# Attention and gated MLP on one core: the first load of q in two halves, the two constants in one, and one store per tile of the last product

## The chip, the core and the metric

The kernel runs on one core of a Trainium2 chip. The metric is the device time of one execution in microseconds (us), as the median of several runs. Three runs of the kernel before gave 281.07, 280.37 and 281.18 us: a median of 281.07.

## What is computed

Eight batches of eight heads, 576 tokens, head width 64. Each head does a linear attention whose features are the positive part of q and k, times a cosine and a sine of the position. The result, 4,608 rows of 512, goes through a two-layer network with the gate h·cos(h).

```python
theta = np.pi / 2.0 * pos / S
phi = concatenate([relu(x) * cos(theta), relu(x) * sin(theta)])    # for q and for k
kv = einsum('bhsf,bhsd->bhfd', k_p, v);  z = sum(k_p, axis=2)
x = (q_p @ kv) / (q_p @ z + 1e-6)       # -> rows of 8 heads x 64
h = x @ w_in                            # 512 -> 2048
out = (h * cos(h)) @ w_out              # 2048 -> 512
```

Inputs and output are float32; the products run on float16 tiles.

## The kernel before

**Tokens.** 576 tokens are four and a half tiles of 128. A batch is therefore read in two pieces (`tokens`, L321): 320 tokens as 64 partitions of five tokens ("five"), and 256 tokens as 64 partitions of four ("four"). The two pieces go to the even and the odd partitions of one tile of 128 partitions (`blocks`, L217). The fifth tokens of all eight batches are collected and form a ninth block of 512 rows. So there are nine blocks, c = 0 to 8; the last is written by `store` and `store_tile` in their branch for c == B.

**The order of the work** is not decided by a scheduler at run time. Each step (a few matmuls, one activation, one DMA) is added to a plan (`Plan.add`). `Plan.run` (L179) sorts the steps by the numbers of a table, `STARTS`, and takes the engine of each from a string, `ENGS`. Each engine then runs its own steps in that order, and waits on semaphores where a tile is written by another engine or by a DMA. The numbers themselves are no times on the chip: only the order that they give counts.

**The start.** `setup` (L1023) issues two small DMAs from ACT: `CS` (L1030), the cosines and sines, 128 partitions of 24 float32, and `IDENT` (L1031), the identity for transposes on TensorE, 128 x 128 float16. SP issues the loads of batch 0 in the order q, k, v (`load`, L330): for q the "four" piece for all eight heads (L340), then the "five" piece (L337), the same for k, and v in two groups of four heads. `prep` (L359) turns a tile of q or k into its features on DVE or ACT, with one column of `CS` as the scale; `q_pe` (L422) transposes on TensorE against `IDENT`. Until there is data TensorE runs warm-up matmuls (`warm`, L1038). A tiny copy on POOL that reads a finished q feature releases the weight loads: first two quarters of w_in (L1071), later the other two, then two quarters of w_out (L1094). The loads of batch 1 wait for the third quarter of w_in through another tiny copy on POOL (`hold_raw`, L1097), and the other two quarters of w_out wait for q of batch 1 (`part_of_w_out`, L1103).

**The middle.** `layer1` does x @ w_in and the gate, `layer2` the product with w_out. For most blocks both are done by a scheme with seven products in place of eight, with sums of the operands made on DVE; L954 is the matmul of `layer2`, L737 that of the fast part of `layer1`.

**The end.** `layer2(8)` (L915) has its last product in two banks of PSUM, one per tile of 128 rows (L1015). Its two results are added to what is there by DVE (L1018, one instruction per tile), the second tile first in the order of the plan, and each is stored by `store_tile` (L859). A tile's 128 partitions hold two batches, 64 partitions each, which lie apart in the output. `store_tile` therefore issues two DMAs for a tile, one from SP and one from ACT, each of 64 partitions x 256 float32 (64 KB). Before them `store` (L824) puts out 512 KB and 256 KB in the same way, half from SP and half from ACT.

Of the kernel before, what the change touches and what calls it, by code (L numbers as in the profile page):

```python
# [17 lines left out]
OPT = dict(F16=0, WS2=[3, 1], HQ=[2, 0, 1], AQ=0, FW=[20, 4, 4, 4, 4], W2F=0, WQ=2, L2F=0, WFI=None, XPE=[0,  # L18
           1, 2, 3, 4], FAST1={3: 2, 4: 2, 5: 2, 6: 4, 7: 4, 8: 4}, MODE={}, HH='', LD=[['k', 0], ['v', 0],
           ['q', 0], ['k', 1], ['v', 1], ['q', 1]], NB=[['A0', 'A1'], ['A0', 'A1', 'M0']], XB=[['B3'], ['B3',  # L20
           'M1']], W0=5, W1=6, WF=[[2, 2, 2, 2], [2, 2, 0, 0]], HOLD=['k', 1], P0=0, RAW1=2, WO2=1, H1=0,
           DA=0, W2=0, SQ=0, NUZ=1)
# [169 lines left out]
def kernel(  # L192
# [9 lines left out]
    nc = tc.nc  # L202
# [32 lines left out]
    def sb(name, shape, dt=F16):  # L235
        return pool.tile(shape, dt, name=name)
# [1231 lines left out]
```

## Time and profile before

| | us |
|---|---|
| median of three runs | 281.07 |
| the profiled execution | 280.38 |
| its span, first to last instruction | 278.5 |
| TensorE busy in it | 271.0 (97%) |
| VectorE (DVE) busy | 236.8 (85%) |
| ScalarE (ACT) busy | 210.2 (75%) |
| GpSimd (POOL) busy | 83.3 (30%) |

The profiled execution is 1.9 us longer than its span, and 0.7 us below the median of the runs. The granted TensorE clock was 0.996. The chain of waits goes back from the last instruction to what released it, step by step, and so lists the pieces that add up to the span. "SPq" and "ACTq" are the issue queues of those engines: a DMA stands there with the time that its issue takes, while its bytes move later. The table of stretches gives, for a stretch of time, the busy time of every engine, the granted clock, the busy share of the 16 DMA engines (a little over 1 where packets overlap) and the bytes moved per second.

### The profile page before, as it was taken

The numbers are of one execution on the slowest core, as the hardware profiler recorded it, in microseconds if no ns is written. First come the engines' busy times: TensorE is split into PE (matmuls) and PEld (weight loads), VectorE is DVE, ScalarE is ACT, GpSimd is POOL, SyncE is SP. The second block draws the span as 40 slices with busy tenths as digits, with TensorE's granted clock in tenths as the row PEclk, the third lists the DMA queues.
The fourth block names the chain that finished last, engine by engine and source line by source line (L and its number), as shares of the span: only waits on it lengthen the run. The fifth ranks groups of instructions, "written<-read, shape, count | busy, mean of one in ns | idle before, by whom it ended". The sixth has DMA issues, their size and how long they took to land.

```text
span 278.5 us, 6813 instructions
## 1 busy us (share of the span) xinstructions
PE 271.0 (97%) x2689; PEld 214.4 (77%) x2689; DVE 236.8 (85%) x442; ACT 210.2 (75%) x363; POOL 83.3 (30%) x104
## 2 busy tenths in 40 slices
PE   8999999999999999999999999999999999999993
PEld 3568766778966677868876878789988888888882
DVE  1886798989999999999999998899989879973952
ACT  2847797979997896888989978995758596777330
POOL 1340020111403001610430045132634372499210
PEclk9999999999999999999999999999999999999998
DMA  6999999999999999969999998939756494698125
GB/s 206 337 206 207 359 230 269 327 311 206 366 253 232 243 259 238 275 209 238 272 269 236 224 259 274 134 88 147 158 75 136 109 166 92 158 141 121 75 78 151
DMA packets 80223, 58.03 MB, mean 208 GB/s; under 512 B 43200, under 2 KB 77248, under 8 KB 80192
## 3 DMA queue, kind: packets, MB, share of 16 engines
q1 hardware_dynamic: 68960, 39.99, 61.1%
q0 software_dynamic: 10496, 17.04, 29.3%
q10 hardware_dynamic: 736, 0.57, 0.7%
q8 instruction: 21, 0.34, 0.5%
q14 instruction: 10, 0.08, 0.1%
HBM read 36.75 MB, written 11.80 MB: 174 GB/s over the span
## 4 chain that ended last, share of the span: by engine, by line
PE 87%; DMA 5%; DVE 3%; ACT 1%; SPq 1%; issue 1%; POOL 0%; DVEq 0%; ACTq 0%
PE M L954 35%; PE M L737 14%; PE M L609 11%; PE TR L737 6%; DMA qm<-in_q_dram 5%; PE M L576 5%; PE M L879 4%; PE ATT L465 3%; PE ATT L398 3%; PE TR L609 2%; PE ATT L1042 1%; DVE KQ L370 1%; PE M L429 1%; ACT ch L548 1%; SPq L340 1%
## 5 line engine op out<-in xcount | busy, mean ns | idle before, releaser
L954 PEld LDWEIGHTS <-gT 128*128 128x128 f16 x560 | 53.9, 98 | 8.3
L954 PE MATMUL M<-w_out_sb,gT 128*128 128x256 f16 x448 | 57.1, 273 | 0.0
L550 DVE TENSOR_TENSOR gT<-M,ch 128x512 f16<-128x512 f32 x73 | 48.5, 685 | 6.6 <-ACT ch L548 6.5
L548 ACT ACTIVATE ch<-M 128x512 f32<-128x512 f32 x75 | 43.4, 596 | 12.1 <-PE M L576 5.0
L369 ACT ACTIVATE KQ<-km,CS 128x512 f16<-128x512 f32 x57 | 38.5, 719 | 0.4 <-DMA km<-in_k_dram 0.4
L965 ACT ACTIVATE ost<-M 128x512 f32<-128x512 f32 x41 | 24.3, 596 | 17.9 <-PE M L954 12.9
L369 ACT ACTIVATE KQ<-qm,CS 128x512 f16<-128x512 f32 x46 | 31.5, 720 | 4.1 <-DMA qm<-in_q_dram 4.1
L609 PE MATMUL M<-xT,w_in_sb 128*128 128x512 f16 x136 | 33.8, 379 | 0.0
L954 PE MATMUL M<-T,S 128*128 128x256 f16 x256 | 32.4, 273 | 0.0
L385 POOL CAST V<-vm 128x1024 f16<-128x1024 f32 (+1 forms) x18 | 15.9, 906 | 50.7 <-DVE den L482 23.8
L737 PEld LDWEIGHTS <-w_in_sb 128*128 128x128 f16 x288 | 27.3, 98 | 4.8 <-issue 0.4
L576 PE MATMUL M<-xT,w_in_sb 128*128 128x256 f16 x256 | 30.4, 273 | 0.2
L954 PEld LDWEIGHTS <-S 128*128 128x128 f16 x256 | 24.8, 98 | 4.1 <-DVE S L930 0.2
L576 PEld LDWEIGHTS <-w_in_sb 128*128 128x128 f16 x256 | 24.4, 98 | 4.1 <-issue 0.5
L749 DVE TENSOR_TENSOR Z<-M,Z 128x512 f32<-128x512 f32 x31 | 21.1, 687 | 4.3 <-PE M L737 3.1
L609 PEld LDWEIGHTS <-w_in_sb 128*128 128x128 f16 x160 | 14.9, 98 | 12.2
L550 POOL TENSOR_TENSOR gT<-Z,ch 128x512 f16<-128x512 f32 x5 | 6.3, 1268 | 56.6 <-ACT ch L548 20.0
L486 DVE TENSOR_TENSOR XN<-ATT,rec 128x512 f16<-128x512 f32 x32 | 22.1, 691 | 1.1
L465 PEld LDWEIGHTS <-qT 128*128 128x128 f16 (+1 forms) x320 | 14.8, 101 | 5.2 <-issue 3.2
L760 ACT ACTIVATE ch<-Z 128x1024 f32<-128x1024 f32 x12 | 12.7, 1057 | 6.9 <-DVE Z L749 4.9
L745 ACT ACTIVATE Z<-M 128x512 f32<-128x512 f32 x26 | 15.1, 596 | 3.4 <-PE M L737 2.4
L370 DVE TENSOR_SCALAR KQ<-qm,CS 128x512 f16<-128x512 f32 x26 | 12.1, 487 | 5.6 <-DMA qm<-in_q_dram 5.6
(152 smaller groups left out, 520.0 us busy)
## 6 DMA issues: line engine op xcount, KB each, us to landing
out_dram<-ost POOLq DMA_DIRECT2D x38, 256.0 KB, 4.3
qm<-in_q_dram SPq DMA_DIRECT2D x8, 640.0 KB, 6.0
km<-in_k_dram SPq DMA_DIRECT2D x8, 640.0 KB, 7.4
qm<-in_q_dram SPq DMA_DIRECT2D x8, 512.0 KB, 6.3
km<-in_k_dram SPq DMA_DIRECT2D x8, 512.0 KB, 6.0
vm<-in_v_dram SPq DMA_DIRECT2D x6, 640.0 KB, 6.1
vm<-in_v_dram SPq DMA_DIRECT2D x6, 512.0 KB, 4.6
w_in_sb<-in_moe_w_in_dram POOLq DMA_DIRECT2D x4, 512.0 KB, 8.1
```

The costliest lines, as they stand in the source:

```text
L369: fn = {"ACT": lambda: nc.scalar.activation(out=out_, in_=in_, func=AF.Relu, scale=sc), "DVE": lambda: nc.vector.tensor_scalar(out=out_, i ...
L385: "POOL": lambda: nc.gpsimd.tensor_copy(out=out_, in_=in_)}
L465: nc.tensor.matmul(bank[hb][ps, hh * D1:(hh + 1) * D1], lhsT=x[:, h, :], rhs=z[:, h, :], start=True, stop=True)
L486: nc.vector.tensor_tensor(out=split(x16[n][:, hs, :], k), in0=A[:, :, :, 0:D], in1=split(rec[n][:, hs], k).unsqueeze(3).broadcast_to((P, k ...
L548: act(0.5, due, lambda: nc.scalar.activation(out=ch[c], in_=bank, func=AF.Sin, bias=math.pi / 2.0, scale=1.0), [key], [("ch", c)])
L550: mul(due, 0.61, lambda q: q.tensor_tensor(out=dst, in0=bank if len(dst.shape) == 2 else bank.rearrange("p (j s) -> p j s", j=dst.shape[1] ...
L576: nc.tensor.matmul(M1[m][:, jj * 2 * P:(jj + 1) * 2 * P], lhsT=w_in_sb[:, cc, j * P:(j + 1) * P], rhs=X[:, cc, ts], start=(cc == 0), stop= ...
L609: nc.tensor.matmul(M, lhsT=w_in_sb[:, cc, j * P:(j + 1) * P], rhs=X[:, cc, :], start=(cc == 0), stop=(cc == NCT - 1))
L737: nc.tensor.matmul(bank[0][:, j * TH:(j + 1) * TH], lhsT=a(cc, j), rhs=b[:, cc, :], start=(first and j == 0 and cc == 0), stop=(last and j ...
L749: dve(0.61, due + 0.3, lambda: nc.vector.tensor_tensor(out=dst, in0=bank[0], in1=dst, op=ALU.add), [bank[1], key], [key])
L954: nc.tensor.matmul(bank[0][:, tt * MH:(tt + 1) * MH], lhsT=a[:, j, tt * P:(tt + 1) * P], rhs=b[:, j, :], start=(first and (apart or tt == ...
L965: act(0.5, due, lambda: nc.scalar.activation(out=dst, in_=view(bank), func=AF.Copy), [bank[1]], dk)
```

## The change

There are three edits, and a table `STARTS` with other numbers for them.

- The cosines, sines and the identity become one tensor, `CONST`, of 128 partitions x 88 float32 (the identity as 64 of them, read as float16), loaded by one DMA. `CS` and `IDENT` are views of it.
- The "four" piece of q of batch 0 is loaded by two DMAs of four heads each (256 KB) in place of one of eight heads (512 KB). The "five" piece follows as before.
- `store_tile` issues one DMA for the 128 partitions of a tile (128 KB), whose destination is two batches x 64 rows x 256. The second tile's goes out from SP, the first tile's from ACT.

The option `L0S` is off, so the new loop over `cuts` in `layer2_plain` has a single cut and does what was there. The new `STARTS` and `ENGS` put the instructions of every engine in the same order as before, but for the DMAs of the three edits: SP issues one more at the start, ACT one fewer at the start, and SP and ACT one fewer each at the end. POOL's queue, with the loads of w_in and w_out in it, has the same entries in the same order.

```diff
-OPT = dict(F16=0, ..., WQ=2, ..., WO2=1, ...)
+OPT = dict(TM=1, CM=0, QS=1, F16=0, ..., L0S=0, ..., WQ=2, ..., WO2=1, ...)
...
-    cs_dr = nc.inline_tensor(cs_np, name="cs_const")
-    ident_dr = nc.inline_tensor(np.eye(P, dtype=np.float16), name="ident_const")
+    CW = cs_np.size // P
+    const_np = np.concatenate([cs_np.reshape(P, -1), np.eye(P, dtype=np.float16).view(np.float32)], axis=1)
+    const_dr = nc.inline_tensor(np.ascontiguousarray(const_np), name="const")
...
-    CS = sb("CS", [P, 2, 2, NT + 2], F32)
-    IDENT = sb("IDENT", [P, P])
+    CONST = sb("CONST", [P, CW + P // 2], F32)
+    CS = CONST[:, 0:CW].rearrange("p (n g t) -> p n g t", n=2, g=2)
+    IDENT = CONST[:, CW:CW + P // 2].bitcast(F16)
...
+            elif b == 0 and nm == "q" and OPT["QS"]:
+                def go4s(h, four):
+                    return lambda: LQ.dma_start(out=blocks(m, 1 - n)[:, h, 0:NT, :], in_=four[:, h])
+                for hs_ in HALVES:
+                    pl.add(LE, LO, 0, due, go4s(hs_, four), (), [(x, 1 - n) for x in part[hs_]],
+                           dma=(nb * NT / 2, 355.0), lane="first", late=LATE_BY[0], lazy=None)
...
     def store_tile(o, i, due):
+        if OPT["TM"]:
+            dst = out.rearrange("(i n s) m -> n i s m", n=2, s=S)[:, 2 + i, 0:S5, 0:MH]
+            put(due, dst.rearrange("n (p t) m -> n p t m", t=NT + 1)[:, :, NT],
+                ost[o][:, i, 0:MH],
+                [("ost", o, 0, i)], *((nc.sync, "SP") if i else (nc.scalar, "ACT")), nb=131.0)
+            return
         for n in range(2):
             dst = out.rearrange("(i n s) m -> n i s m", n=2, s=S)[n][2 + i, 0:S5, 0:MH]
...
-        nc.scalar.dma_start(out=CS, in_=cs_dr.ap())
-        nc.scalar.dma_start(out=IDENT, in_=ident_dr.ap())
+        nc.scalar.dma_start(out=CONST, in_=const_dr.ap())
```

More of the change, by code (lines that the diff above doesn't have):

```diff
@@ L15 @@
 SYNC = mybir.DependencyInfo(mybir.DependencyClass.Sync, mybir.DependencyReason.DATA)
[L18 to L22, printed above, removed]
@@ L25 @@
-STARTS = (
[98 rows of a table removed]
+OPT = dict(TM=1, CM=0, QS=1, F16=0, WS2=[3, 1], HQ=[2, 0, 1], AQ=0, L0S=0, FW=[20, 4, 4, 4, 4], W2F=0, WQ=2,
+           L2F=0, WFI=None, XPE=[0, 1, 2, 3, 4], FAST1={3: 2, 4: 2, 5: 2, 6: 4, 7: 4, 8: 4}, MODE={}, HH='',
+           LD=[['k', 0], ['v', 0], ['q', 0], ['k', 1], ['v', 1], ['q', 1]], NB=[['A0', 'A1'], ['A0', 'A1',
+           'M0']], XB=[['B3'], ['B3', 'M1']], W0=5, W1=6, WF=[[2, 2, 2, 2], [2, 2, 0, 0]], HOLD=['k', 1],
+           P0=0, RAW1=2, WO2=1, H1=0, DA=0, W2=0, SQ=0, NUZ=1)
@@ L124 @@
+STARTS = (
[98 rows of a table added]
 )
 ENGS = (
-    "DDPPPPPSSSSSSSSDAPDDDPADAPDDAPAGGGGDADADDDADADADADDADADGGGGGGPPADPPDPPAPPDPPAPPDPPAPPDPA"
-    "PADPADPADPADPADPADPADPADPADPADPADPADPADPADPADPADGSSGSSGGGGGSSSSDADADADADADAPDDAPADAPDDAP"
-    "ADADADADDADADPPAPPDPAPPDPAPPDPAPPDPAPDPPDPAPAPAPAPAPDPDGGPDPDGGPADPADPADPADPADPADPADPADP"
-    "ADPADPADPADPADPADPADPADDDDDSSSSSSADADAADDAAGGGPPADASDDSAASAASPPDPAPPDPAPPDPAPPDPADDDPPAP"
-    "PDDPPAPPAPPDPPDGGPPAGGPADPADPADPADPADPADPADPADPADPADPADPADPADPADPADPADSSSSSSDDAAAAAAAAGG"
@@ L131 @@
-    "GPPADASAASDASAASADPPDSPPDSPPDSPPDSSPPDSDDDDDDDPPAPPDDPPAPPAPPDPPDGGPPAGGDDDDPAPDAGPAPAPD"
-    "PDADPADPADPADPADPADPAPDAGPAPAPDPDADPADPADPADPADPADSSSSSSAAAAAADAAAGGGPPAAASAASAASADSPPDS"
-    "PPDSPPDSPPDSDDDPPAPPDDPPAPPAPPDPPDGGPPAGGDDDDPAPDAGPAPAPDPDADPADPADPADPADPADPAPDADPAPAPD"
-    "PDADPADPADPADPADPADSSSSSSDDAAAAAAADGGGPPAADSAASDDSAASAAPPDSPPDSPPDSPPDSSPPDSDDDPPAPPADPP"
-    "AGGPPAPPAPPAGGPPAGGGGDDDDPAPDAGPAPAPDPDADPADPADPADPADPADPAPDADPAPAPDPDAGPADPADPADPADPADS"
-    "SSSSSAAAAAAADAAGGGPPAAASADSADSAASPPDSPPDSPPDSPPDSDDDDDDDPPAPPADPPAGGPPAPPAPPAGGPPAGGGGDD"
@@ L137 @@
-    "DDPAPDADPAPAPDPDADPADPAPDAGPAPAPDPDAGPADPAPDADPAPAPDPDADPADPAPDADPAPAPDPDADPADSSSSSSDAAA"
-    "AAAAAAGGGPPADASDASAASDDSAAPPDSPPDSPPDSPPDSSPPDSDDSPPAPPAGGPPAGGPPAPPAPPAGGPPAGGGGDDDDPAP"
-    "DAGPAPAPDPDAGPADPAPDADPAPAPDPDADPADPAPDADPAPAPDPDADPADPAPDADPAPAPDPDADPADDDDDSPPAPPDGGPP"
-    "APPAPPDPPDGGPPAGGDDDDPAPDAGPAPAPDPDAGPADPAPDAGPAPAPDPDAGPADPAPDAGPAPAPDPDADPADPAPDAGPAPA"
-    "PDPDADPADDDDDDDPPAPPDDDPPAPPAPPDPPDSASAAPPDSADSA"
+    "DDPPPPPSSSSSSSSSDAPDDDPADAPDDAPAGGGGDADADDDADADADADDADADGGGGGGPPADPPDPPAPPDPPAPPDPPAPPDP"
@@ new lines @@
+    "APADPADPADPADPADPADPADPADPADPADPADPADPADPADPADPADGSSGSSGGGGGSSSSDADADADADADAPDDAPADAPDDA"
+    "PADADADADDADADPPAPPDPAPPDPAPPDPAPPDPAPDPPDPAPAPAPAPAPDPDGGPDPDGGPADPADPADPADPADPADPADPAD"
+    "PADPADPADPADPADPADPADPADDDDDSSSSSSADADAADDAAGGGPPADASDDSAASAASPPDPAPPDPAPPDPAPPDPADDDPPA"
+    "PPDDPPAPPAPPDPPDGGPPAGGPADPADPADPADPADPADPADPADPADPADPADPADPADPADPADPADSSSSSSDDAAAAAAAAG"
+    "GGPPADASAASDASAASADPPDSPPDSPPDSPPDSSPPDSDDDDDDDPPAPPDDPPAPPAPPDPPDGGPPAGGDDDDPAPDAGPAPAP"
+    "DPDADPADPADPADPADPADPAPDAGPAPAPDPDADPADPADPADPADPADSSSSSSAAAAAADAAAGGGPPAAASAASAASADSPPD"
@@ new lines @@
+    "SPPDSPPDSPPDSDDDPPAPPDDPPAPPAPPDPPDGGPPAGGDDDDPAPDAGPAPAPDPDADPADPADPADPADPADPAPDADPAPAP"
+    "DPDADPADPADPADPADPADSSSSSSDDAAAAAAADGGGPPAADSAASDDSAASAAPPDSPPDSPPDSPPDSSPPDSDDDPPAPPADP"
+    "PAGGPPAPPAPPAGGPPAGGGGDDDDPAPDAGPAPAPDPDADPADPADPADPADPADPAPDADPAPAPDPDAGPADPADPADPADPAD"
+    "SSSSSSAAAAAAADAAGGGPPAAASADSADSAASPPDSPPDSPPDSPPDSDDDDDDDPPAPPADPPAGGPPAPPAPPAGGPPAGGGGD"
+    "DDDPAPDADPAPAPDPDADPADPAPDAGPAPAPDPDAGPADPAPDADPAPAPDPDADPADPAPDADPAPAPDPDADPADSSSSSSDAA"
+    "AAAAAAAGGGPPADASDASAASDDSAAPPDSPPDSPPDSPPDSSPPDSDDSPPAPPAGGPPAGGPPAPPAPPAGGPPAGGGGDDDDPA"
@@ L142 @@
+    "PDAGPAPAPDPDAGPADPAPDADPAPAPDPDADPADPAPDADPAPAPDPDADPADPAPDADPAPAPDPDADPADDDDDSPPAPPDGGP"
+    "PAPPAPPDPPDGGPPAGGDDDDPAPDAGPAPAPDPDAGPADPAPDAGPAPAPDPDAGPADPAPDAGPAPAPDPDADPADPAPDAGPAP"
+    "APDPDADPADDDDDDDPPAPPDDDPPAPPAPPDPPDSASAAPPDADS"
 )
@@ L875, in layer2_plain, with mm @@
                 M, mk = BANKS_L2[jh][n % len(BANKS_L2[jh])]
-                def mm(M=M, t=t, js=js):
-                    for j in js:
-                        nc.tensor.matmul(M, lhsT=G[:, j, t * P:(t + 1) * P], rhs=w_out_sb[:, j, :],
-                                         start=(j == js[0]), stop=(j == js[-1]))
-                pe(len(js), MM, due, mm,
-                   [("g", c % 2, j, t) for j in js]
-                   + [("w_out", g) for g in range(4 * js[0] // NJT, 4 * js[-1] // NJT + 1)], [mk])
+                cuts = [js[i:i + 4] for i in range(0, len(js), 4)] if OPT["L0S"] and jh else [js]
+                for jp in cuts:
+                    def mm(M=M, t=t, jp=jp, js=js):
+                        for j in jp:
+                            nc.tensor.matmul(M, lhsT=G[:, j, t * P:(t + 1) * P], rhs=w_out_sb[:, j, :],
+                                             start=(j == js[0]), stop=(j == js[-1]))
+                    pe(len(jp), MM, due, mm,
+                       [("g", c % 2, j, t) for j in jp] + ([mk] if jp[0] != js[0] else [])
+                       + [("w_out", g) for g in range(4 * jp[0] // NJT, 4 * jp[-1] // NJT + 1)], [mk])
                 o = os_[t // 2]
```

196 rows, old and new, of the table STARTS are left out of this document.

## The prediction

> **What bounds the kernel now.** I read the page's busy table first, then the chain of waits, then the table of stretches at both ends, since the three edits touch only the first 15 us and the last 6.
>
> The page's first lines, and pieces of the chain (start, us, what):
>
> ```profile
> span 278.5 us, 6813 instructions
> PE 271.0 (97%) x2689; PEld 214.4 (77%) x2689; DVE 236.8 (85%) x442; ACT 210.2 (75%) x363; POOL 83.3 (30%) x104
> ```
>
> ```profile
> 1.56 5.58 DMA qm<-in_q_dram
> ...
> 27.12 9.59 DMA qm<-in_q_dram
> ...
> 258.10 13.99 PE M L954 x128
> ...
> 273.46 0.81 DVE ost L1018 x2
> ```
>
> TensorE carries the span. After 38 us the list of TensorE's waits holds two entries of 0.4 and 0.2 us, so from there to 272.1 us only fewer matmuls would help, and the change keeps them all. Two DMA waits come before (q of batch 0, landing at 7.1; q of batch 1, landing at 36.7), and behind the last addition come the stores. The start, in the table of stretches (columns: stretch, length, five engines, clock, share of the DMA engines, GB/s):
>
> ```profile
> 1.50:2.25 0.75, 0.75 (x3) 0.25 (x2) 0.48 (x1) 0.64 (x1) 0.00 (x0) 1.00 0.18 16
> 2.25:2.50 0.25, 0.25 (x2) 0.05 (x1) 0.00 (x0) 0.25 (x1) 0.00 (x0) 1.00 1.17 115
> 2.50:3.25 0.75, 0.75 (x3) 0.30 (x2) 0.00 (x0) 0.60 (x2) 0.00 (x0) 1.00 0.64 83
> 3.25:6.50 3.25, 3.25 (x9) 1.14 (x8) 0.00 (x0) 0.00 (x0) 0.00 (x0) 1.00 1.06 358
> ...
> 12.50:28.00 15.50, 14.84 (x174) 11.21 (x172) 12.03 (x34) 9.88 (x19) 4.02 (x10) 1.00 1.24 212
> 28.00:36.75 8.75, 8.75 (x72) 6.88 (x71) 6.69 (x12) 7.09 (x13) 0.00 (x0) 1.00 1.08 361
> ```
>
> The DMA engines ramp up until 3.25 us and have no gap from there to 36.75 (the stretches left out read 1.08 and 1.09). Both waits for q thus end when the bytes ahead have gone through: a ramp that ends d earlier brings d, an issue that stays ahead of its bytes brings nothing. The end:
>
> ```profile
> 273.92 1.21 SPq L822 DMA_DIRECT2D out_dram<-ost  x2
> 273.92 1.41 ACTq L822 DMA_DIRECT2D out_dram<-ost  x2
> ...
> 275.25:275.75 0.50, 0.00 (x0) 0.00 (x0) 0.00 (x0) 0.00 (x0) 0.00 (x0) 1.00 1.03 350
> 275.75:276.50 0.75, 0.00 (x0) 0.00 (x0) 0.00 (x0) 0.00 (x0) 0.00 (x0) 0.72 0.98 306
> 276.50:276.75 0.25, 0.00 (x0) 0.00 (x0) 0.00 (x0) 0.00 (x0) 0.00 (x0) 0.50 0.38 123
> 276.75:278.50 1.75, 0.00 (x0) 0.00 (x0) 0.00 (x0) 0.00 (x0) 0.00 (x0) 0.50 0.00 0
> ```
>
> The last bytes leave at about 276.6 (31 KB in the last stretch, at 306 GB/s). Then 1.9 us pass with no bytes, for the receipt and the program's end; this stays. Nothing covers the store: what it takes longer, the kernel takes longer.
>
> **The start, part by part.** *q in halves.* The issue of "four" took 0.76 us (0.74 to 1.50); issues of four heads (v, L340) took 0.64. So the first half is issued by 1.38, the second by 2.06, and "five" begins at 2.10 in place of 1.56. Everything behind it in SP's queue (k, v) goes out 0.55 later; the last v issue goes from 5.60 to about 6.15, and its bytes, behind some 3.2 MB at 357 GB/s, are not due before 12. "Five" is due when the 524 KB of "four" are through. The stretches, less 44 KB of constants, put that at about 4.7; issued at 2.10, it needs 1.2 us to its first bytes by the stores at the end (issued 271.14, bytes from 272.35), or 2.5 by q's own first DMA (0.74 to 3.25): 3.3 to 4.6. The cover is thin at one end; without it the loss is the whole 0.55. The gain is at most 0.12, the shorter first issue. The first q features wait for three loads of q in place of two, and still for "five".
>
> *One constant.* ACT issues one DMA less (0.44 us). The table load and a warm-up activation behind it are done at 3.1, and ACT then idles to 7.24. `CONST` is due at 7.24, too; the two old DMAs landed 1.7 and 3.7 us after their issue, so by 4.9, which leaves 2.4 us of cover. The DMA engines lose 128 of 256 rows. The stretch 1.50 to 2.25, with mostly the rows of `CS`, is 0.18 x 0.75 x 16 = 2.2 us of engine time, 0.14 us over 16 engines; that is the most to be had, and in a stretch in which they were mostly idle. I take 0 for the start, between -0.3 (both gains) and +0.55.
>
> **The end, part by part.** The order stays: second tile from SP, then first tile from ACT. The first store is issued at 273.92 as now. The other needs the second addition, done at 274.27, so it goes out at 274.32 in place of 274.51 and 274.53, where it stood behind the first pair: 0.2 us earlier. Bytes follow 1.2 later, at 275.1 and 275.5.
>
> How fast they go is the question. The 16 engines each moved 350 / 16 = 21.9 GB/s in 275.25 to 275.75, which is 47 ns for a row of 1 KB. The four stores of now (64 KB each) have 64 partitions outermost on both sides, and so does, with 64 or 128, every other plain load and store of this kernel: counts that divide by 16. The new store is the only one whose destination begins with a count of two, 2 x 64 x 256, against 128 x 256 in its source. Two ends, then. If its 128 rows are dealt out over 16 engines, it costs what the pair did. If a transfer is cut along its outermost dimension, the destination can be cut in two: two engines with 64 rows each. No row of the trace has such a DMA. The nearest in bytes, the 128 KB halves of `store` (landing 3.4 and 3.6 us after issue), have 64 outermost and can't decide. I take the two engines: the rows that show 16 engines at work all have an outermost count that 16 divides, and this store has lost just that.
>
> In the Trainium skill, "DMA: Bandwidth & Descriptors", the section "Why a DMA increments its semaphore by 16 and not by 1" states this rule: the number of engines is the largest up to 16 that divides the slowest dimension of both sides, and a DMA from SP or ACT takes the lowest-numbered ones. By it both stores run on the same two engines; no run here shows that yet. The table "Rules for kernel authors" on the same page speaks for the change, advising one transfer of 128 partitions in place of two halves; by that alone the end would gain the 0.2 us of issue.
>
> The sum for two engines, the same for both stores. At 275.1 the stretches have moved 580 of 1,049 KB; of the other 469, 262 are the two tiles, and 207 are older stores, 13 rows of 1 KB for each engine. Each of the two engines then has 13 + 2 x 64 = 141 rows: at 47 ns 6.6 us, to 281.7. That is 5.1 past 276.6; I take 5.0. At the best rate of loads (396 GB/s in the stretch 30 to 31, 41 ns a row) it is 5.8 us and +4.3; at 306 GB/s (54 ns) 7.6 us and +6.1. With the profiled execution's 280.38: 280.38 + 0 + 5.0 = **285.4**, and 284.4 to 286.6 by the ends. That execution is 0.7 below the median of the runs shown, so a median may come out as far above; 0.3% of this kernel, 0.84 us, is what a measurement can tell from no change.
>
> **Rivals.**
> - *16 engines after all: not slower.* Place: the last two stores. The 469 KB left at 275.1 go at 350 GB/s in 1.34 us, to 276.45: 0.15 earlier than now. For it: the same bytes, rows and first issue as today. Against it: the outermost two. Time 280.38 - 0.15 - 0.1 for the ramp = 280.1, and 279.8 to 280.9 with the start's bounds. The point from which it decides: 262 KB on n engines at 21.9 GB/s, from 275.7, end within 0.84 us of 276.6 if n is at least 7.
> - *Two engines for each store, but not the same two.* Each has 77 rows, 3.6 us; the later starts at 275.5 with some 9 old rows, to 278.9, or +2.3: 282.7. For it: the stores come from different queues. Against it: nothing in the trace ties an engine to a queue.
> - *The start loses its cover*, with 16 engines at the end: "five" 0.55 late and the stream with it, 280.8; only with a longer first latency over 281.9.
> - *The change doesn't do what it says.* Its title speaks of two quarters of w_out ahead of batch 1. They already go ahead of it (WO2 and WQ stay), and POOL's order is the same, so this part is worth nothing in every case.
>
> **How the numbers follow.** Same two engines 0.56 (285.4), two pairs 0.05 (282.7), 16 engines 0.36 (280.1), lost cover beyond 0.84 us 0.03. Slower by over 0.3%: 0.56 + 0.05 + 0.03 = 0.64. Of the 0.36, 0.08 goes to faster by over 0.3% (ramp gain at its bound and a little more), 0.28 to within. The range must reach the second case to leave out no more than 2 in 10: 279.9 to 286.6, with 284.4 to 286.6 as the likeliest's own.
>
> **What would show it.** Two engines: a share of DMA engines near 0.13 and some 40 to 50 GB/s in the stretches after about 276, for 5 us; landings of about 5 and 8 us for the two stores. Two pairs: a share near 0.25 for 3 us. 16 engines: shares near 1 to the end, and landings below 3.6. For the start: q landing within 0.3 us of 7.1 and the first transposes with it, and no gap in the stretches between 3.25 and 36.75; "five" late would show as a share well under 1 near 4.5. The forecast is wrong if the row time on two engines is far from 47 ns, or if the cut follows the source.

## The result, and the profile after

| | before | after |
|---|---|---|
| median, us (six runs each, same chip) | 281.12 | 288.48 |
| lowest to highest | 280.37 to 281.62 | 287.85 to 290.05 |
| the profiled execution | 280.38 | 290.05 |
| its span | 278.5 | 288.1 |
| q of batch 0 landed | 7.14 | 9.37 |
| last addition begins | 273.46 | 277.66 |
| TensorE clock granted | 0.996 | 0.991 |

The changed kernel takes 1.027 times as long, 95% interval [1.024, 1.0301]: 7.4 us slower, 1.9 us above the top of the range. Its profiled execution was the slowest of its six, so it shows the costs large. Its mean clock is lower because its idle end, at 0.50, is longer. Ranges and ratios further down leave out two disturbed executions, one of 472 us (`e4_const`) and one of 571 us (`e5_half_on_act`). The head of its page, which has the same work in a longer span:

```profile
span 288.1 us, 6811 instructions
PE 271.7 (94%) x2689; PEld 213.9 (74%) x2689; DVE 237.0 (82%) x442; ACT 210.0 (73%) x363; POOL 83.4 (29%) x104
```

The chain of waits (start, us, what) has the same pieces as before, and tells where the 9.6 us of span came in:

```profile
2.23 7.14 DMA qm<-in_q_dram
...
29.00 10.70 DMA qm<-in_q_dram
...
262.29 13.99 PE M L970 x128
...
277.66 0.81 DVE ost L1034 x2
```

q of batch 0 lands 2.2 us later, q of batch 1 3.0 later (39.7), the last matmuls and the last addition 4.2 later. From the last matmul to the end of the span it is 11.8 us in place of 6.4. So there are two losses: 4.2 us ahead of the last matmul, and 5.4 behind it. TensorE's list of waits has most of the first: behind the initial 1.3 us its waits add up to 4.8 us in place of 1.2, and 2.8 of them, in place of 0.6, are the transposes' waits for features.

*The start.* SP's queue (start, us):

```profile
0.74 1.45 SPq L350 DMA_DIRECT2D qm<-in_q_dram  x2
2.23 0.61 SPq L339 DMA_DIRECT2D qm<-in_q_dram  x1
```

The two halves take 0.76 and 0.62 us to issue: the first is no shorter than that of the whole was, and "five" goes out at 2.23 in place of 1.56. The table of stretches (length, five engines, clock, DMA share, GB/s) of the changed kernel:

```profile
4.00:4.50 0.50, 0.50 (x3) 0.16 (x2) 0.00 (x0) 0.00 (x0) 0.00 (x0) 1.00 1.23 274
4.50:5.00 0.50, 0.50 (x2) 0.15 (x1) 0.00 (x0) 0.00 (x0) 0.00 (x0) 1.00 0.64 164
5.00:5.50 0.50, 0.50 (x2) 0.15 (x1) 0.00 (x0) 0.00 (x0) 0.00 (x0) 1.00 0.89 310
```

In the kernel before the last two columns of these stretches read 1.12 and 373, 1.09 and 392, 1.05 and 392. The stream that had no gap now has one at 4.5. The trace's single rows show how it comes about. "Four" begins its last row at 4.30 in place of 4.82, since the stream got going faster: 378 KB had moved by 3.5, in place of 218. "Five" begins its first row at 4.00 in place of 4.53, 1.8 us after its issue. Its first 32 rows take 102 ns each in the mean, in place of 55, and a later one takes 1.72 us. The 16 counts of its landing, one from each DMA engine, show the rest: in the kernel before the last came 0.37 us after the first; now 14 are there by 7.00, and the last two come at 8.59 and 9.37.

*The end*, in the same table:

```profile
279.50:280.00 0.50, 0.00 (x0) 0.00 (x0) 0.00 (x0) 0.00 (x0) 0.00 (x0) 1.00 0.86 293
280.50:281.00 0.50, 0.00 (x0) 0.00 (x0) 0.00 (x0) 0.00 (x0) 0.00 (x0) 1.00 0.00 0
281.50:282.00 0.50, 0.00 (x0) 0.00 (x0) 0.00 (x0) 0.00 (x0) 0.00 (x0) 1.00 0.14 49
285.00:285.50 0.50, 0.00 (x0) 0.00 (x0) 0.00 (x0) 0.00 (x0) 0.00 (x0) 0.50 0.14 49
286.50:287.00 0.50, 0.00 (x0) 0.00 (x0) 0.00 (x0) 0.00 (x0) 0.00 (x0) 0.50 0.08 29
```

The older stores go out at a share near 1. Then for about a microsecond only four rows move, of 0.43 to 0.60 us each (a row counts in the stretch in which it begins, hence the 0.00). From 281.5 to 286.8 the share is 0.14. Of 16 engines that is 2.2: two engines, with 49 GB/s between them, 24.5 each, or 42 ns for a row of 1 KB. Both stores are under way in this time, so two engines for each would show 0.25. In the trace each merged store has three counts where the other stores have 16: one within 0.4 us of the end of its issue, which must stand for 14, and two when it lands, the last at 286.01 and 287.19.

### The profile page after: what moved, and what is told of

Its sections match the earlier page's. It is cut to its first block, busy times and chain, and to the rows that moved or that the text cites. A ratio compares the mean times of both kernels' runs of the same rounds, so it can differ in the third digit from the quotient of the medians.

```text
span 288.1 us, 6811 instructions
## 1 busy us (share of the span) xinstructions
PE 271.7 (94%) x2689; PEld 213.9 (74%) x2689; DVE 237.0 (82%) x442; ACT 210.0 (73%) x363; POOL 83.4 (29%) x104
## 4 chain that ended last, share of the span: by engine, by line
PE 81%; DMA 9%; ACT 2%; DVE 2%; SPq 1%; issue 1%; DVEq 0%
PE M L970 32%; PE M L745 13%; PE M L617 9%; DMA qm<-in_q_dram 6%; PE M L584 6%; PE TR L745 6%; PE M L895 4%; PE ATT L473 3%; PE ATT L406 3%; DMA qT<-KQ 2%; PE TR L617 1%; PE ATT L1057 1%; DVE KQ L378 1%; PE M L437 1%; ACT ch L556 1%; ACT KQ L377 1%
## 5 line engine op out<-in xcount | busy, mean ns | idle before, releaser
L377 ACT ACTIVATE KQ<-km,CONST 128x512 f16<-128x512 f32 x57 | 38.5, 719 | 1.2 <-DMA km<-in_k_dram 1.2
L377 ACT ACTIVATE KQ<-qm,CONST 128x512 f16<-128x512 f32 x46 | 31.5, 720 | 6.8 <-DMA qm<-in_q_dram 6.8
L378 DVE TENSOR_SCALAR KQ<-qm,CONST 128x512 f16<-128x512 f32 x26 | 12.1, 486 | 7.9 <-DMA qm<-in_q_dram 7.8
```

Of the source, the lines that this page charges most:

```text
L377: fn = {"ACT": lambda: nc.scalar.activation(out=out_, in_=in_, func=AF.Relu, scale=sc), "DVE": lambda: nc.vector.tensor_scalar(out=out_, i ...
```

## The experiments

Theory: the merged stores run on two engines because their destination begins with two; and q is late because "five" goes out 0.67 us later, the DMA engines run dry, and restart unevenly. Rivals: the stores pay for their size or their queue; q pays for the split itself, or through TensorE's clock. Ratios are to the kernel before on the same chip, with 95% intervals. All these kernels compute the whole of the reference.

### Undoing one edit, and one edit alone

The changed kernel with the old four stores (`e1_pairs`):

```diff
-OPT = dict(TM=1, CM=0, QS=1, ...)
+OPT = dict(TM=0, CM=0, QS=1, ...)
```

> The changed kernel with the old store of two DMAs of 64 partitions per tile; split q and one constant stay. Theory (the merged store runs on two DMA engines and costs 5.4 us, the profiles' stretch from the end of the matmuls to the end of the span being 11.8 against 6.4 us; the split of q costs the remaining 2): 283 us, and a DMA share near 1 up to the last bytes. Rival (the store costs all of the 7.4 us, and the late q of the profiled execution is chance): 281.1 us, q landing near 7.1 us in the profile.

282.23 (281.39 to 284.19), ratio 1.005 [1.0029, 1.0071]: +1.4 us.

The kernel before with the merged stores alone (`e2_store`):

```diff
+OPT = dict(TM=1, CM=0, QS=0, ...)
...
+            dst = out.rearrange("(i n s) m -> n i s m", n=2, s=S)[:, 2 + i, 0:S5, 0:MH]
+            put(due, dst.rearrange("n (p t) m -> n p t m", t=NT + 1)[:, :, NT],
+                ost[o][:, i, 0:MH],
+                [("ost", o, 0, i)], *((nc.sync, "SP") if i else (nc.scalar, "ACT")), nb=131.0)
+            return
```

> The kernel before with the merged store alone. Theory: 281.1 + 5.4 = 286.5 us, with some 5 us of a DMA share near 0.13 and 45 to 50 GB/s at the end, and q landing at 7.1 us as before. Rival (the store costs it all): 288.5 us.

286.69 (286.16 to 287.33), ratio 1.0203 [1.0174, 1.0233]: +5.7 us. The tail, in its table of stretches:

```profile
277.00:278.00 1.00, 0.00 (x0) 0.00 (x0) 0.00 (x0) 0.00 (x0) 0.00 (x0) 1.00 0.13 8
279.00:280.00 1.00, 0.00 (x0) 0.00 (x0) 0.00 (x0) 0.00 (x0) 0.00 (x0) 0.50 0.13 47
```

The first of these lines holds the slow first rows, the second the same two engines' share as in the changed kernel, with the old start (q landed at 7.33).

The kernel before with q in halves alone (`e3_q`):

```diff
+OPT = dict(TM=0, CM=0, QS=1, ...)
...
```

> The kernel before with q's first load in two halves alone. Theory (the five-token piece is issued 0.66 us later and the DMA engines run out of work near 4.5 us): 283 us, with a stretch well under a full share between 4 and 5.5 us and q landing 1 to 2 us later than 7.1. Rival (the constant did it, or chance): 281.1 us.

283.78 (283.48 to 284.52), ratio 1.0103 [1.0071, 1.0135]: +2.9 us. q landed at 9.10, and its table has the gap too:

```profile
4.50:5.00 0.50, 0.50 (x4) 0.26 (x3) 0.00 (x0) 0.00 (x0) 0.00 (x0) 1.00 0.51 125
5.00:5.50 0.50, 0.50 (x4) 0.20 (x3) 0.00 (x0) 0.00 (x0) 0.00 (x0) 1.00 0.64 172
```

The kernel before with the one constant alone, timed (`e4_const`), and once more for a profile (`e12_const_look`):

```diff
...
-        nc.scalar.dma_start(out=CS, in_=cs_dr.ap())
-        nc.scalar.dma_start(out=IDENT, in_=ident_dr.ap())
+        nc.scalar.dma_start(out=CONST, in_=const_dr.ap())
```

> The kernel before with the one constant alone. Theory (no cost: it lands long before it is used): 281.1 us, between 280.8 and 281.4. Rival (its rows of 352 bytes or its place ahead of q's rows hold back some DMA engines): 283 us, with q landing later than 7.1 us.

> The kernel before with the one constant alone, for a profile. Theory: q landing at 7.1 to 7.5 us, all 16 engines within 0.9 us, no dip between 3.5 and 5.5 us, 280.4 to 281.6 us. Rival: a dip or a spread over 1 us.

Ratio 1.0001 [0.9986, 1.0017]; the profiled execution took 280.90, with q landed at 6.86 and no gap (393 GB/s from 4.5 to 5.0).

What follows: the stores cost 5.7, the constant nothing, and the split is the rest, 1.4 us beside the constant and 2.9 alone. 5.7 + 1.4 = 7.1, of 7.4 measured; the intervals cover the other 0.3.

### The store: what makes it slow

The same two DMAs of 128 KB, cut the other way: each holds 64 partitions, outermost, of both tiles (`e8_store_by_half`):

```diff
-            store_tile(oh, i, d + 1.0)
+        for n in range(2):
+            dst = out.rearrange("(i n s) m -> n i s m", n=2, s=S)[n][2:4, 0:S5, 0:MH]
+            put(d + 1.0, dst.rearrange("i (p t) m -> p t i m", t=NT + 1)[:, NT], ost[oh][n * R:(n + 1) * R, :, 0:MH], ...)
```

> The kernel before with two stores in place of four at the end, as many and as large as in the change (128 KB), but cut the other way: 64 partitions with both tiles each, so that the outermost count is 64 on both sides and not 2. Both wait for the second addition. Theory (the number of engines follows the outermost count): a DMA share near 1 to the last bytes, 281.0 us, within 0.4 of the kernel before. Rival (one 128 KB store per queue is slow whatever its shape): 284 to 287 us.

281.46, ratio 1.0018 [0.999, 1.0047]: the loss is gone, with as few and as large DMAs as in the changed kernel. Its last stretches keep nearly all engines busy:

```profile
277.00:278.00 1.00, 0.00 (x0) 0.00 (x0) 0.00 (x0) 0.00 (x0) 0.00 (x0) 1.00 0.83 268
278.00:279.00 1.00, 0.00 (x0) 0.00 (x0) 0.00 (x0) 0.00 (x0) 0.00 (x0) 1.00 0.70 203
```

So it isn't the size of the stores, nor their number; it is the count that stands outermost.

Only the second tile's store merged (`e10_one_tile`), to tell one pair of engines from two:

```diff
-        if OPT["TM"]:
+        if OPT["TM"] and i == 1:
```

> The kernel before with the merged store for the second tile only; the first tile keeps its two DMAs of 64 partitions. Theory (both merged stores run on the same two engines, one row of 1 KB after the other, 42 ns each): 64 rows in place of 128, so half of the cost, 281 + 2.7 to 3.2 = 284 us. Rival (each store has engines of its own, and the cost is that of one store): 286.5 us, as with both.

284.6, ratio 1.0105 [1.007, 1.014]: +3.0, half of the 5.7. With a pair of engines for each store the second would have run beside the first, and one alone would have cost nearly what both do. The stores from SP and from ACT share the same two engines, as the share of 0.14 with both under way has it too. The share in this run:

```profile
280.00:281.00 1.00, 0.00 (x0) 0.00 (x0) 0.00 (x0) 0.00 (x0) 0.00 (x0) 0.50 0.13 44
```

Both merged stores from POOL (`e11_store_from_pool`):

```diff
-                [("ost", o, 0, i)], *((nc.sync, "SP") if i else (nc.scalar, "ACT")), nb=131.0)
+                [("ost", o, 0, i)], nc.gpsimd, "POOL", nb=131.0)
```

> The kernel before with the merged store of both tiles issued from POOL's queue, not from SP and ACT. Theory (the cut follows the outermost count on every queue): again two engines, 286 to 288 us. Rival (only SP's and ACT's queues cut that way; POOL's deals 128 partitions over 16 engines): a share near 1 to the last bytes, 281 to 282.5 us with its later first bytes.

288.25, ratio 1.0244 [1.0203, 1.0285]: a little above the time that theory gave, and another shape.

```profile
278.00:279.00 1.00, 0.00 (x0) 0.00 (x0) 0.00 (x0) 0.00 (x0) 0.00 (x0) 1.00 0.27 27
280.00:281.00 1.00, 0.00 (x0) 0.00 (x0) 0.00 (x0) 0.00 (x0) 0.00 (x0) 0.50 0.31 71
```

For a time the share is twice that of two engines, each store has all of its 16 counts (the second's lie between 280.59 and 283.93), and the span goes on for 3.2 us after the last count, in place of 1.3 in the kernel before. The counts alone would say 16 engines; the rows say otherwise. POOL's stores go out as 64 rows of 4 KB. Until 279.4 no more than two of them are in flight at once, from 279.8 to 281.6 mostly four, and from 282.1 on two again. So from POOL, too, each store runs on two engines, but the second store's are not the first's. The two stores overlap only from 279.4 to 282.1, and the longer end behind them stays open.

### The start: the split, the delay, or the clock

The halves at the same time from two engines, so that "five" goes out at 1.56 as before (`e5_half_on_act`; the lines taken out are the changed kernel's):

```diff
-                for hs_ in HALVES:
-                    pl.add(LE, LO, 0, due, go4s(hs_, four), ...)
+                first.append(lambda: nc.scalar.dma_start(out=blocks(m, 1 - n)[:, HALVES[1], 0:NT, :], in_=four[:, HALVES[1]]))
+                pl.add(LE, LO, 0, due, go4s(HALVES[0], four), ...)
```

> The kernel before with q's four-token piece in two halves, the first issued from SP and the second from ACT at the same time, ahead of the constants, so that the five-token piece is issued at 1.56 us as before. Theory (the cost of the split is the later issue of the five-token piece behind it, which lets the DMA engines run out of work near 4.5 us): no dip between 4 and 5.5 us, q landing near 7.1 us, 280.8 to 281.2 us. Rival (two smaller transfers, or one more of them, cost by themselves): near 283.8 us, as with both halves on SP.

282.13 (280.79 to 282.61), ratio 1.0026 [1.0004, 1.0048]. No gap (387 GB/s from 4.5 to 5.0), q landed at 7.09. The split with "five" in time costs 0.7 us and not 2.9, though theory had it at no cost.

No split, but "five" late: both constants (`e6_five_later`), or `CS` alone (`e7_five_little_later`), go out on SP between "four" and "five":

```diff
             def go5(h=h, five=five):
+                if b == 0 and nm == "q":
+                    nc.sync.dma_start(out=CS, in_=cs_dr.ap())
+                    nc.sync.dma_start(out=IDENT, in_=ident_dr.ap())
                 LQ.dma_start(out=blocks(m, n)[:, h], in_=five)
```

> The kernel before, q not split, but with the DMAs of the cosines and of the identity moved from ACT to SP, between q's four-token and five-token pieces, which then goes out some 0.9 us later, at about 2.45. Theory: the same dip as with the split, q landing 1 to 2.5 us later, 282.5 to 284 us. Rival (splitting costs, not the delay): 281 us.

> The kernel before, q not split, with the DMA of the cosines alone between q's two pieces on SP: the five-token piece some 0.4 us later, at about 1.95. Theory (its first bytes come 2.7 us after its issue, as in the changed kernel's profile, and the four-token piece lasts to about 4.7): just in time, no dip or a faint one, 281 us and at most 0.4 above the kernel before. Rival (any delay is paid in full from the first tenth): 281.3 us or more, growing with the delay.

"Five" went out at 2.68 and 2.21. 282.38, ratio 1.0051 [1.0032, 1.0071], and 282.51, ratio 1.0053 [1.0029, 1.0078]. In the second I had taken 0.4 us for the issue of `CS`, and it took 0.60, so this is not the small delay that it was meant to be; it is the delay of the change, without the split. Both have the gap, the first:

```profile
4.50:5.00 0.50, 0.50 (x2) 0.15 (x1) 0.00 (x0) 0.00 (x0) 0.00 (x0) 1.00 1.22 156
5.00:5.50 0.50, 0.50 (x2) 0.15 (x1) 0.00 (x0) 0.00 (x0) 0.00 (x0) 1.00 0.43 79
```

The delay alone makes the gap and costs 1.4 to 1.5 us, as much as the split with one constant. In these stretches the engines are slow as much as idle: the share of 1.22 goes with only 156 GB/s, since a row of "five" takes up to 1.02 us.

The split as in the change, with other bytes to move in the gap: k's first piece goes out from ACT at the start (`e9_split_filled`):

```diff
-            if b == 0 and nm == "q" and OPT["AQ"]:
-                first.append(go4)
+            if b == 0 and nm == "k":
+                first.append(lambda: nc.scalar.dma_start(out=blocks(m, 1 - n)[:, h, 0:NT, :], in_=four))
```

> The kernel before with q's four-token piece in two halves on SP, as in the change, so that the five-token piece is issued at 2.23 us, and with k's four-token piece issued from ACT at the start, which gives the DMA engines 512 KB more to do meanwhile. Theory (engines that run dry start again with rows of 0.4 to 1.7 us; it is the dry spell, not the late issue, that costs): no dip under a share of 0.9 between 4 and 5.5 us, the 16 engines' parts of the five-token piece landing within 0.6 us of each other, though later (about 8.2 us, since k's bytes go first); 281 to 282.3 us. Rival (the late issue itself): landings spread over 1 to 3 us, 282.5 to 284 us.

283.23, ratio 1.0059 [1.0028, 1.009]: the rival's time, not theory's. The gap is gone (379 GB/s from 4.5 to 5.0), and q still lands at 9.31, now behind k's bytes ("five" went out at 2.45 in this run). So it doesn't tell what the restart costs; it shows that a q made late in another way costs 1.7 us too.

In the two dearest of these, `e3_q` and `e9_split_filled`, there is something else. TensorE's list and the stretches of `e3_q`:

```profile
10.17 0.62 PE L435 MATMUL M<-IDENT,KQ 128*128 128x128 f16 x8 [2.94 <-DVE KQ L376]
```

```profile
11.00:12.00 1.00, 0.95 (x10) 0.99 (x11) 0.29 (x1) 1.00 (x2) 0.37 (x2) 0.53 1.07 382
12.00:13.00 1.00, 1.00 (x10) 0.85 (x9) 0.90 (x2) 0.68 (x2) 0.90 (x2) 0.50 1.09 366
```

The warm-up matmuls ended 2.94 us before the first transposes, and from 11.1 to 14.5 the granted clock, the column ahead of the share, is 0.50. In `e9_split_filled` the pause was 3.06. In the changed kernel it was 2.03 and the clock stayed at 1.00. I formed a third theory from this, "clock", and changed the number of warm-ups: 28 in place of 20 in `e3_q`, `e9_split_filled` and the changed kernel, and 8 in place of 20 in the kernel before:

```diff
-FW=[20, 4, 4, 4, 4]
+FW=[28, 4, 4, 4, 4]
```

> Split of q alone, with 28 warm-up matmuls on TensorE in place of 20 ahead of the first transposes. Theory "clock": in the split alone TensorE had 2.94 us of nothing ahead of its first transposes (warm-ups ended at 7.23, transposes began at 10.17), and its granted clock then was 0.50 from about 11.1 to 14.3; 3.2 us at half speed is 1.6 us of work. Eight more matmuls of 0.22 to 0.43 us shorten the pause to about 1 us, the clock stays at 1.00 and the time falls from 283.8 to about 282.2, that of the split with one constant. Rival "late landing alone": the 283.8 is the price of q's late bytes whatever TensorE does meanwhile, so it stays at 283.8.

> Split of q with k's first piece issued from ACT at the start, and 28 warm-up matmuls in place of 20. Theory "clock": the run with 20 had a pause of 3.06 us on TensorE and a clock of 0.50 from 11.2 to 14.5; with the pause down to about 1 us the time falls from 283.2 to about 281.7. Rival "late landing alone": 283.2 as before.

> The kernel before with 8 warm-up matmuls in place of 20, and nothing else: q lands as early as before (7.1). Theory "clock": the 8 matmuls end at about 4.8, TensorE then has 3.4 us of nothing until its first transposes at 8.2, the granted clock goes to 0.50 for some 3 us behind them, and the time rises by about 1.5 us, to 282.4. Rival "late landing alone": q's landing is unchanged, so the time stays at 280.9.

> The changed kernel with 28 warm-up matmuls in place of 20. Its profile had a pause of 2.03 us on TensorE and a granted clock of 1.00 behind it, so with the clock already kept nothing is to be had: 288.5. If other runs of it lost the clock as the split alone did, the median falls by up to 1.5, to 287.0. Rival "late landing alone": 288.5 in any case.

| warm-ups changed | median | ratio | the same with 20 |
|---|---|---|---|
| q alone | 283.44 | 1.007 [1.0043, 1.0098] | 1.0103 |
| q alone, filled | 283.12 | 1.007 [1.0043, 1.0097] | 1.0059 |
| before, 8 | 282.17 | 1.0036 [1.001, 1.0063] | 1 |
| changed kernel | 287.96 | 1.0244 [1.0216, 1.0272] | 1.027 |

In the first two the clock stayed at 1.00, q landed as late as before (9.66 and 9.44), and the time did not fall to 282: "clock" fails as the main reason why these two are dear, and "late landing alone" holds within its intervals. A part of 0.9 us in the split alone isn't excluded, since its two intervals overlap. The changed kernel's 0.5 us lies within its intervals too. A slow clock is worth something by itself: with q in time and 8 warm-ups, the kernel before lost 1.0 us. TensorE's list of `e15_before_less_warm`:

```profile
1.32 3.60 PE L1042 MATMUL ATT<-S 128*128 128x512 f16 x8 [1.32 <-POOL S L1024]
8.22 1.89 PE L429 MATMUL M<-IDENT,KQ 128*128 128x128 f16 x16 [3.31 <-DVE KQ L370]
10.76 1.89 PE L1042 MATMUL ATT<-S 128*128 128x512 f16 x4
```

Four warm-ups behind the transposes took 1.89 us, and 1.03 in the kernel before. This is not the clock lost in the pause of 3.31 us that the theory spoke of: the 8 warm-ups ahead of it took 0.45 us each, as slow as those four, and the trace's first record of the clock, at 1.00, begins at 12.51 in place of 6.42. What the run shows is a full clock that came 6 us later. The clock column reads 1.00 where there is no record, so the durations have to be read beside it.

Put side by side, the profiled executions of the kernels with the old stores, sorted by q's landing, say what the start costs:

| | q landed, us | execution, us |
|---|---|---|
| one constant (`e12_const_look`) | 6.86 | 280.90 |
| half on ACT (`e5_half_on_act`) | 7.09 | 281.30 |
| before | 7.14 | 280.38 |
| split, one constant (`e1_pairs`) | 7.41 | 281.39 |
| `CS` between (`e7_five_little_later`) | 7.71 | 281.15 |
| split, clock lost (`e3_q`) | 9.10 | 283.85 |
| both constants between (`e6_five_later`) | 9.22 | 283.07 |
| filled, clock lost (`e9_split_filled`) | 9.31 | 283.61 |
| filled, 28 warm-ups (`e14_filled_more_warm`) | 9.44 | 283.01 |
| split, 28 warm-ups (`e13_q_more_warm`) | 9.66 | 283.33 |

q lands either by 7.7 or after 9.1, and the time follows it: the five early ones take 281.0 us in the mean, the five late ones 283.4, for a landing some 2 us later. With the same kernel and "five" at 2.2 both seem to happen: the runs of `e1_pairs` spread from 281.39 to 284.19, and the profiled one, with q in time, is the fastest. The single rows tell the kernels with the gap from those without: taking the time that rows on SP's queue spent above 60 ns each between 3.8 and 6.5 us, it adds up over the engines to 0.4 us before and at most 3.3 in the kernels without the gap, and to between 7.2 and 11.9 us in those with it, where single rows took up to 1.75 us. They don't tell a late landing from an early one: `e1_pairs` and `e7_five_little_later` have 7.2 and 7.8 us of slow rows and landed by 7.7. That depends on the slowest engines: between the first and the last count of "five" lie 0.9 and 1.1 us in these two, and 1.9 to 3.2 in the others with the gap.

What stays open: why rows are slow behind a gap, why the split alone costs more than the split with one constant (2.9 against 1.4 us), and why "half on ACT" still costs 0.7. One execution doesn't fit the table: that of `e8_store_by_half` took 282.59, at the upper end of its runs, with q landed at 7.51. None of these kernels beats the kernel before.

## Why the prediction was wrong in size

The time came out 3.1 us above the 285.4. Of these 1.4 are the start, 0.7 the end, and 0.7 the base: the sum began at the profiled execution, 280.38, and the median of the kernel before is 281.12. The prediction said that a median may lie that much higher, and left it out of the sum and the range. The other 0.3 aren't told apart.

**The end, +5.0: right in its mechanism and close in size.** The store alone measured +5.7, and 5.4 from the last matmul to the end in the profile. Two engines, the same two for both queues, as forecast. Two terms were off and partly cancel: a row took 42 ns, not 47, which alone gives +4.4 by the same sum; and there is a stop of about 1.2 us before the merged stores flow, which the sum did not have. Their first rows took 0.15 to 0.6 us each in the trace, 0.046 after that. The step that failed a little is "bytes follow 1.2 later, at 275.1 and 275.5", which took it that the two engines would then run at the stream's rate. The landings were to come about 5 and 8 us after issue; they came after 7.9 and 8.6.

**The start, 0: the term of the sum that was mis-sized, and the largest part of the miss.** Measured: +1.4 beside the one constant, +2.9 alone, 2.2 us of late landing in the profile. Three parts of that step failed.
- "The first half is issued by 1.38." An issue of half the bytes took the same 0.76 us, so "five" went out at 2.23 and not at 2.10.
- "It needs 1.2 us to its first bytes ... or 2.5 by q's own first DMA: 3.3 to 4.6." I kept both ends and then priced by the early one. The sign that the prediction named for a late "five" came out, a share well under 1 near 4.5 (0.64). "Five" showed its first row 1.8 us after its issue, between the two ends, at 4.00. What the step had wrong is the other side: it put the end of "four" at about 4.7, near the kernel before's 4.87, and in the changed kernel's profile, where the stream got going faster, it came at 4.35. What the step counted as a gain shortened the cover, and the rival "the start loses its cover" was worth far more than 0.03.
- "Without it the loss is the whole 0.55." This took a stream that stops to go on where it stopped. In the changed kernel's trace the rows behind the gap were slow on some engines, up to 1.72 us each, and the last engine decides when q has landed: 2.2 us late for 0.67 us of delay. Nothing in the trace of before bounded this upward. The range didn't even hold the step's own bound: its upper end, 286.6, had 0.1 us of start loss in it, and with the whole 0.55 it is 287.0.

**One constant, 0: right** (1.0001). In its one profile q landed 0.28 us earlier, near the most that the prediction allowed for the faster start, and the time didn't follow.

**The w_out quarters, 0: right.** None of the three edits touches them, POOL's order was the same, and the parts measured add up without them.

**Rivals.** "16 engines after all", to which I gave 0.36, is refuted by the share of 0.14 and by the cut by halves, which did get them. "Two engines for each store" is refuted for SP and ACT by the single merged tile at half the cost, and by the share of 0.14 with both stores under way; from POOL it is what the rows show.

The Trainium skill, "DMA: Bandwidth & Descriptors", section "Why a DMA increments its semaphore by 16 and not by 1", has the rule by which two outermost entries give two engines: for the stores from SP and ACT the runs agree (share 0.14, and three counts in place of 16); for the same stores from POOL they agree as well, with two rows in flight for each store. The advice of one transfer of 128 partitions in the section "Rules for kernel authors" does not hold for this one, which cost 5.7 us; the measurement decides.

## What to carry to other kernels

When DMAs are merged, look at what stands outermost on both sides: put a count that 16 divides there, as the 64 of `e8_store_by_half`, even if that means cutting the other way. When a load is split at the start of a kernel, count the issue time of every piece, and ask when the next one's first bytes come by the slowest latency seen at that place, and whether the edit also lets the bytes ahead of it end sooner; an issue 0.67 us later, at a place where the stream ran dry, cost 1.4 to 2.9 us here. And where a loss has no cover and no row to price it, its upper end belongs in the range.

## What the runs showed of the hardware

- The time to issue a DMA did not follow its size: 0.76 us for the first on SP whether it carried 512 or 256 KB, then 0.60 for `CS` with 12 KB and 0.42 for `IDENT` with 32.
- The first rows behind a gap were slow: 0.15 to 0.6 us each for the merged stores, which then took 0.046, and up to 1.75 us for rows of "five", which took 0.055 in the kernel before.
- A pause of TensorE of 2.94 or 3.06 us was followed by 3.4 us at a granted clock of 0.50, which began 0.8 to 0.9 us after the pause; pauses of 0.93 to 2.03 were not. The Trainium skill, "TensorE: Matmul & The Clock Gate", section "What's actually happening", states a window of about 3.4 us that doesn't start with the kernel; pauses a little shorter than that were enough here. With 8 warm-ups in place of 20 the full clock came at 12.51 us in place of 6.42, at a price of 1.0 us of this kernel.
- From POOL the merged stores used two engines each, and not the same two; it was no faster (+6.9 against +5.7), and the span went on for 3.2 us behind the last count.
